# Moving the transposes of an attention kernel from TensorE to the DMA crossbar, and V's loads to another queue

## The chip, the cores and the metric

One core of a Trainium2 chip. The metric is the device time of one execution in microseconds (us). Each kernel was run several times, and the median is quoted. Runs that were flagged slow (over 1.5% above the fastest of the same kernel) are named where they occur and are left out of the ratios.

## The reference

Causal attention in which 16 extra "beacon" keys come before the 576 keys of each head, and then a two-layer MLP over all 4,608 tokens.

```python
B, H, S, Nb, D = 8, 8, 576, 16, 64          # q, k, v: [B, H, S, D], float32
k_all = concatenate([beacon_k, k], axis=2)
v_all = concatenate([beacon_v, v], axis=2)
scores = q @ k_all.T / sqrt(D)              # causal mask on the 576 keys only
a = softmax(scores)
x = (a @ v_all)  -> [B * S, H * D] = [4608, 512]
h = x @ w_in                                # 512 -> 2048
out = maximum(0.01 * h, h) @ w_out          # 2048 -> 512
```

## The kernel before

The program interleaves two kinds of work on TensorE. A *step* handles one pair of heads (32 pairs: 8 batches of 4): scores, exponentials on ScalarE, the product with V. *Fills* are pieces of the MLP that have their data already (MoE pieces). The order of each engine's instructions is fixed by the program; where an engine waits in the traces below, its later instructions wait too (DVE once for 24 us).

Q, K and the attention output must be transposed. Before, TensorE does that by multiplying with an identity, and DVE (VectorE) copies the result from PSUM, the memory into which TensorE writes, to SBUF, from which TensorE reads:

```python
def t_q(g, which, copy=nc.vector.tensor_copy):      # Q or K of pair g
    ...
    for i in range(RI):                              # 9 transposes
        nc.tensor.transpose(ps[:, i*RP:(i+1)*RP], nat[b, grp][which][ps_, i]..., ident[ps_, ps_])
    copy(out=dst..., in_=ps[:, 0:S]...)

def x_transposes(g):                                 # the attention output of pair g
    for t, (q0, rows) in enumerate(QT):              # 5 transposes
        nc.tensor.transpose(ps[:, q0:q0+rows], x_nat[0:rows, t]..., ident[0:rows, 0:rows])
    nc.vector.tensor_copy(out=xT[:, hp, b*S:(b+1)*S], in_=ps[:, 0:S])
```

The data comes in like this. Pool (GpSimd) issues the loads of Q and K and permutes them; SP issues V's loads and the stores of the result. Batch 2's loads stand behind 8 MB of MLP weights, and the step of pair 8 (the first of batch 2) has 16 extra fills ahead of its first transposes to cover that delay:

```python
def load_v(b, after=None):
    first = nc.sync.dma_start(out=t[0:NB, 0], in_=beacon_v[b]...)      # six DMAs on SP
    ...
def loads(g):
    ...
    if b > 1:
        if hp == 0: load_v(b + 1)
        if hp < 2:  load_qk(b + 1, hp)                 # Pool: 4 loads per group
    if hp >= 2:
        permute(b + 1, hp - 2, 0 and 1, Pool)
    if hp == 3: cast_v(b + 1, nc.gpsimd)
...
if g == 2 * NPAIR:                                     # pair 8
    ... finish(g - 1)
    for n in range(16): fill()
    t_q(g, 0); t_q(g, 1)
    ...
```

The softmax here doesn't subtract the row's maximum and nothing guards it: scores larger than these inputs give would overflow.

## Time and profile before

| | before |
|---|---|
| time, median of 4 runs | 375.11 us (374.99 to 377.84) |
| profiled span | 373.4 us |
| TensorE busy | 352.3 us, 94% |
| mean granted TensorE clock | 0.971 |

The page's rows below are those that the prediction does not show. The first gives each engine's busy time, its share of the span and its instructions; the other is the busy share of the DMA engines in 40 slices of the span, in tenths.

```profile
span 373.4 us, 7670 instructions
...
PE 352.3 (94%) x3215; PEld 186.8 (50%) x3264; DVE 172.3 (46%) x399; ACT 197.0 (53%) x311; POOL 101.3 (27%) x143
...
DMA  8998999939157900197017901100010011001012
```

TensorE is the bound. The DMA row has the shape that matters later: full for the first 75 us, and then a burst of one to three slices in each batch (the 7 9, 1 9 7, 1 7 9) with slices near zero between. In windows of the trace, the columns are the window, its length, the busy time of PE, PEld, DVE, ACT and POOL with instruction counts, the clock, the DMA share (the time of all packets over that of 16 engines; it can pass 1, because packets overlap) and GB/s.

```profile
48.00:75.00 27.00, 26.79 (x221) 13.81 (x223) 8.14 (x21) 13.37 (x22) 15.05 (x21) 1.00 1.17 210
...
205.00:219.00 14.00, 13.89 (x133) 7.08 (x133) 6.46 (x17) 11.04 (x20) 2.17 (x2) 1.00 0.70 127
```

In both windows TensorE is busy for all but 0.2 us or less at full clock, although the DMA engines are full in the first.

### The profile page before, as it was taken

Reading aid. Unit: us, or ns where it says so; the run is one execution under the profiler, and the core shown is the slowest. Engines: PE = TensorE matmul, PEld = TensorE weight load, DVE = VectorE, ACT = ScalarE, POOL = GpSimd, SP = SyncE. Lnnn points to the kernel's source line nnn. Section 1 sums busy time; section 2 is a strip of 40 time slices with the busy share of each in tenths; the row PEclk is TensorE's granted clock in tenths of the full one; section 3 lists DMA queues with packets and bytes.
Section 4 is the critical chain, followed back from the end, with each engine's and each line's share of the span. In section 5 each row is a group of like instructions: output and inputs, shape, how many; then the busy total and the mean of one; then the engine's idle time right before and its main releaser. Section 6 shows DMA issues by size and latency. Waiting matters only on the chain.

```text
span 373.4 us, 7670 instructions
## 1 busy us (share of the span) xinstructions
PE 352.3 (94%) x3215; PEld 186.8 (50%) x3264; DVE 172.3 (46%) x399; ACT 197.0 (53%) x311; POOL 101.3 (27%) x143
## 2 busy tenths in 40 slices
PE   5779899999998999999999999999999999999996
PEld 4456564445554555555554455455545554444442
DVE  3699750354558445654455535644554342000021
ACT  4949845476435773378535763587337701643300
POOL 8568127686014702370208101300000000000000
PEclk9558999999999999999999999999999999999999
DMA  8998999939157900197017901100010011001012
GB/s 173 172 221 128 200 203 203 223 81 155 56 126 174 177 0 30 58 152 135 2 59 131 184 2 57 58 2 2 36 50 31 0 58 58 0 5 53 28 56 84
DMA packets 58370, 33.82 MB, mean 91 GB/s; under 512 B 41440, under 2 KB 53472, under 8 KB 58336
## 3 DMA queue, kind: packets, MB, share of 16 engines
q0 software_dynamic: 13152, 13.34, 22.8%
q1 hardware_dynamic: 44896, 19.67, 21.4%
q8 instruction: 25, 0.41, 0.4%
q10 hardware_dynamic: 288, 0.33, 0.3%
q14 instruction: 9, 0.07, 0.1%
HBM read 37.22 MB, written 9.44 MB: 125 GB/s over the span
## 4 chain that ended last, share of the span: by engine, by line
PE 85%; DVE 6%; DMA 3%; POOL 2%; issue 2%; SPq 1%; ACT 0%; POOLq 0%
PE acc L385 33%; PE acc L369 33%; PE av L333 7%; PE sc L267 6%; PE tp L244 4%; PE tp L355 2%; DMA v_raw<-in_k_dram 1%; DMA v_raw<-in_v_dram 1%; DVE xT L360 1%; DVE osb L394 1%; DVE x_nat L343 1%; SPq L216 1%; DVE qT L249 1%; POOL k_raw L137 1%; DVE v_aug L225 1%
## 5 line engine op out<-in xcount | busy, mean ns | idle before, releaser
L369 PE MATMUL acc<-xT,w_in_sb 128*128 128x512 bf16 x552 | 137.6, 379 | 4.0 <-DVE xT L360 2.6
L278 ACT ACTIVATE aT<-sc 128x928 bf16<-128x928 f32 (+2 forms) x128 | 102.4, 856 | 71.4 <-PE sc L267 71.2
L385 PE MATMUL acc<-w_out_sb,gT 128*128 128x512 bf16 x551 | 134.5, 379 | 1.5 <-issue 0.8
L376 ACT ACTIVATE gT<-acc 128x512 bf16<-128x512 f32 x144 | 85.6, 599 | 81.9 <-PE acc L369 79.9
L369 PEld LDWEIGHTS <-w_in_sb 128*128 128x128 bf16 x576 | 52.3, 98 | 59.7 <-issue 4.5
L385 PEld LDWEIGHTS <-gT 128*128 128x128 bf16 x576 | 52.0, 98 | 59.9 <-issue 4.8
L394 DVE COPY osb<-acc 128x512 f32<-128x512 f32 x36 | 24.9, 690 | 95.6 <-PE acc L385 93.6
L333 PEld LDWEIGHTS <-aT 128*128 128x128 bf16 (+1 forms) x960 | 38.6, 100 | 19.0 <-issue 4.7
L267 PE MATMUL sc<-qT,kT 64*128 64x128 bf16 (+5 forms) x384 | 42.1, 306 | 5.0 <-ACT aT L278 2.6
L333 PE MATMUL av<-v_aug,aT 128*128 128x65 bf16 (+1 forms) x960 | 41.8, 197 | 2.5 <-DVE v_aug L225 1.9
L167 POOL COPY q_nat<-q_raw 128x1152 bf16<-128x1152 bf16 (+1 forms) x16 | 18.8, 1176 | 80.3 <-PE tp L244 69.2
L249 DVE COPY qT<-tp 128x576 bf16<-128x576 bf16 x32 | 24.2, 756 | 34.0 <-PE tp L244 33.9
L343 DVE TENSOR_TENSOR x_nat<-av,rec 128x384 bf16<-128x384 f32 x64 | 31.4, 491 | 2.2
L225 POOL CAST v_aug<-v_raw 128x512 bf16<-128x512 f32 (+1 forms) x30 | 19.0, 670 | 35.3 <-PE av L333 34.1
L360 DVE COPY xT<-tp 128x576 bf16<-128x576 bf16 x32 | 14.5, 452 | 29.3 <-PE tp L355 29.3
L267 PEld LDWEIGHTS <-kT 64*128 64x128 bf16 (+1 forms) x384 | 17.4, 100 | 20.5 <-issue 13.5
L342 DVE RECIPROCAL rec<-av 128x6 f32<-128x6 f32 x64 | 11.9, 185 | 29.9 <-PE av L333 29.9
L137 POOL DMA_DIRECT2D q_raw<-in_q_dram x31 | 19.4, 627 | 12.1 <-DMA v_raw<-in_v_dram 4.5
L299 DVE TENSOR_TENSOR aT<-aT,mask 128x768 bf16<-128x768 bf16 x32 | 21.1, 661 | 2.3 <-ACT aT L278 2.3
L137 POOL DMA_DIRECT2D k_raw<-in_k_dram x31 | 19.6, 631 | 8.4 <-DMA w_out_sb<-in_moe_w_out_dram 5.0
L249 DVE COPY kT<-tp 128x576 bf16<-128x576 bf16 x28 | 21.0, 749 | 0.0
L167 POOL COPY k_nat<-k_raw 128x1152 bf16<-128x1152 bf16 (+1 forms) x16 | 18.6, 1164 | 0.3 <-DMA k_raw<-in_k_dram 0.3
(33 smaller groups left out, 152.4 us busy)
## 6 DMA issues: line engine op xcount, KB each, us to landing
out_dram<-osb SPq DMA_DIRECT2D x36, 256.0 KB, 2.0
v_raw<-in_v_dram SPq DMA_DIRECT2D x24, 256.0 KB, 5.6
q_raw<-in_q_dram POOLq DMA_DIRECT2D x31, 144.0 KB, 6.0
k_raw<-in_k_dram POOLq DMA_DIRECT2D x31, 144.0 KB, 6.5
w_in_sb<-in_moe_w_in_dram POOLq DMA_DIRECT2D x4, 512.0 KB, 8.8
w_out_sb<-in_moe_w_out_dram POOLq DMA_DIRECT2D x4, 512.0 KB, 16.8
v_raw<-in_v_dram SPq DMA_DIRECT2D x8, 224.0 KB, 4.5
v_raw<-in_v_dram SPq DMA_DIRECT2D x8, 160.0 KB, 5.0
```

Source lines behind the costliest of these rows:

```text
L137: dma = nc.gpsimd.dma_start(out=dst[e * RP : (e + 1) * RP], in_=src[b, h0 : h0 + 2].rearrange("h (p i) d -> p h i d", i=RI),)
L167: copy(out=dst[p0:p1], in_=src[p0:p1].rearrange("p h i d -> p i h d"))
L225: eng.tensor_copy(out=dst[0 : ROWS[c], c, :, 0:D], in_=t[0 : ROWS[c], c])
L249: copy(out=dst.rearrange("c (p i) -> c p i", i=RI), in_=ps[:, 0:S].rearrange("c (i p) -> c p i", i=RI),)
L267: nc.tensor.matmul(out=sc[0 : ROWS[c], par, col - c0 : col - c0 + w], lhsT=kT[ps_, c * 128 : c * 128 + ROWS[c]], rhs=qT[ps_, q0 : q0 + w], ...
L278: last = nc.scalar.activation(out=aT[:, :, c0 : c0 + w], in_=sc[:, :, 0:w], func=AF.Exp, scale=0.125)
L333: nc.tensor.matmul(out=avv[:, n, 0 : D + 1], lhsT=aT[0 : ROWS[c], par, a0 : a0 + 128], rhs=va[0 : ROWS[c], c, 2 * hp + par, :], start=(c = ...
L343: nc.vector.tensor_tensor(out=x_nat[:, t0:t1].rearrange("p t e d -> p (t e) d"), in0=avv[:, :, 0:D], in1=rec[:, n0:n1, None].to_broadcast( ...
L369: nc.tensor.matmul(out=acc, lhsT=w_in_sb[:, j, fc * 128 : (fc + 1) * 128], rhs=xT[:, j, i * 512 : (i + 1) * 512], start=(j == 0), stop=(j ...
L376: nc.scalar.activation(out=gT[i][:, fc, :], in_=acc, func=AF.Prelu, alpha=0.01)
L385: nc.tensor.matmul(out=acc, lhsT=gT[i][:, fc, t * 128 : (t + 1) * 128], rhs=w_out_sb[:, fc, :], start=(fc == 0), stop=(fc == NF - 1),)
L394: nc.vector.tensor_copy(out=osb, in_=acc)
```

## The change

The intent is to take 522 transposes off TensorE. From batch 2 on, Q and K are transposed by DMAs through the crossbar (they transpose on the way from SBUF to SBUF), issued by SP right after Pool's permutes, into SBUF tiles from which DVE copies; so is the attention output of the first three pairs of each of these batches. V of batches 3 to 7 is loaded by ScalarE's queue, so that SP is free for the crossbar DMAs. The core of the diff:

```diff
-    def load_v(b, after=None):
+    def load_v(b, after=None, queue=nc.sync):
...
+    def turn_pairs(b, grp):
+        for which, name in enumerate(("q_turn", "k_turn")):
+            t = turnpool.tile([128, RI, 2, RP], BF16, name=name)
+            nc.sync.dma_start_transpose(out=t..., in_=nat[b, grp][which]...)
+        turned[b, grp] = tiles
+
+    def in_order(g, eng):
+        eng.tensor_copy(out=kT[:, 0:NB], in_=bkT[:, b, hp])
+        for t, dst in zip(turned[b, grp], (qT, kT[:, NB : NB + S])):
+            eng.tensor_copy(out=dst..., in_=t[:, :, e]...)
...
+    def x_turn(g):
+        nc.sync.dma_start_transpose(out=dst[:, None, 0:112], in_=flat[0:112, 0])
+        nc.sync.dma_start_transpose(out=dst[:, 112:496]..., in_=flat[:, 1:4]...)
+        nc.sync.dma_start_transpose(out=dst[:, None, 448:576], in_=flat[:, 4])
...
-                        load_v(b + 1)
+                        load_v(b + 1, queue=nc.scalar)
...
                     for which in range(2):
                         permute(b + 1, hp - 2, which, nc.gpsimd.tensor_copy)
+                    turn_pairs(b + 1, hp - 2)
...
+            if g + 1 >= 2 * NPAIR and has(g + 1):
+                in_order(g + 1, nc.vector)        # at the head of step g
...
-            x_transposes(g)
+            if b < 2 or hp == NPAIR - 1:
+                x_transposes(g)
+            else:
+                x_turn(g)
...                                                # and the t_q calls from pair 8 on are gone
```

The diff also changes numbers of buffers, which are not shown: four to three for the raw Q and K, three to two for the permuted ones, two to three for the attention output.

More of the change, by code (lines that the diff above doesn't have):

```diff
@@ L69 @@
     rawpool = ctx.enter_context(tc.tile_pool(name="rawpool", bufs=2))
-    qkpool = ctx.enter_context(tc.tile_pool(name="qkpool", bufs=4))
-    natpool = ctx.enter_context(tc.tile_pool(name="natpool", bufs=3))
+    qkpool = ctx.enter_context(tc.tile_pool(name="qkpool", bufs=3))
+    natpool = ctx.enter_context(tc.tile_pool(name="natpool", bufs=2))
+    turnpool = ctx.enter_context(tc.tile_pool(name="turnpool", bufs=2))
     headpool = ctx.enter_context(tc.tile_pool(name="headpool", bufs=2))
@@ L205, in behind @@
         )
-    def load_v(b, after=None):
+    def load_v(b, after=None, queue=nc.sync):
         t = rawpool.tile([128, NKB, H, D], FP32, name="v_raw")
         v_raws[b] = t
-        first = nc.sync.dma_start(out=t[0:NB, 0], in_=beacon_v[b].rearrange("h p d -> p h d"))
+        first = queue.dma_start(out=t[0:NB, 0], in_=beacon_v[b].rearrange("h p d -> p h d"))
         if after is not None:
             behind(first, after)
-        nc.sync.dma_start(out=t[NB:128, 0], in_=v[b, :, 0:112].rearrange("h p d -> p h d"))
+        queue.dma_start(out=t[NB:128, 0], in_=v[b, :, 0:112].rearrange("h p d -> p h d"))
         for c in (1, 2, 3, 4):
-            last = nc.sync.dma_start(
+            last = queue.dma_start(
                 out=t[0 : ROWS[c], c],
@@ L252, in t_q @@
         )
+    turned = {}
+    def turn_pairs(b, grp):
+        tiles = []
+        for which, name in enumerate(("q_turn", "k_turn")):
+            t = turnpool.tile([128, RI, 2, RP], BF16, name=name)
+            nc.sync.dma_start_transpose(
+                out=t.rearrange("c i e p -> c i (e p)"),
+                in_=nat[b, grp][which].rearrange("r i h d -> r (i h d)"),
+            )
+            tiles.append(t)
+        turned[b, grp] = tiles
+    def in_order(g, eng):
+        b, hp = divmod(g, NPAIR)
+        grp, e = divmod(hp, 2)
+        qT = headpool.tile([128, S], BF16, name="qT")
+        kT = headpool.tile([128, NB + S], BF16, name="kT")
+        eng.tensor_copy(out=kT[:, 0:NB], in_=bkT[:, b, hp])
+        for t, dst in zip(turned[b, grp], (qT, kT[:, NB : NB + S])):
+            eng.tensor_copy(
+                out=dst.rearrange("c (p i) -> c p i", i=RI),
+                in_=t[:, :, e].rearrange("c i p -> c p i"),
+            )
+        qk[g] = [qT, kT]
     probs = {}
@@ L319, in value @@
             xs[g] = (
-                headpool.tile([128, 5, 2, D], BF16, name="x_nat"),
+                headpool.tile([128, 5, 2, D], BF16, name="x_nat", bufs=3),
                 headpool.tile([128, 10], FP32, name="rec"),
@@ L360, in x_transposes @@
         nc.vector.tensor_copy(out=xT[:, hp, b * S : (b + 1) * S], in_=ps[:, 0:S])
+    def x_turn(g):
+        b, hp = divmod(g, NPAIR)
+        x_nat, _ = xs.pop(g)
+        flat = x_nat.rearrange("p t e d -> p t (e d)")
+        dst = xT[:, hp, b * S : (b + 1) * S]
+        nc.sync.dma_start_transpose(out=dst[:, None, 0:112], in_=flat[0:112, 0])
+        nc.sync.dma_start_transpose(
+            out=dst[:, 112:496].rearrange("p (t q) -> p t q", t=3),
+            in_=flat[:, 1:4].rearrange("p t x -> p (t x)"),
+        )
+        nc.sync.dma_start_transpose(out=dst[:, None, 448:576], in_=flat[:, 4])
     gT = {}
@@ L519 @@
                     fill()
-                t_q(g, 0)
-                t_q(g, 1)
-                fill()
-                fill()
                 score(g, 0)
@@ L528 @@
                 fill()
-                t_q(g + 1, 0)
-                t_q(g + 1, 1)
                 score(g, 2)
@@ L579 @@
             slot(3)
-            if has(g + 1) and g + 1 != 2 * NPAIR:
-                t_q(g + 1, 0)
-                t_q(g + 1, 1)
             if has(g):
```

## The prediction

> **What bounds the kernel now.** I read the page first: the rows by slice and the chain that ended last.
>
> ```profile
> PE   5779899999998999999999999999999999999996
> ACT  4949845476435773378535763587337701643300
> PEclk9558999999999999999999999999999999999999
> PE 85%; DVE 6%; DMA 3%; POOL 2%; issue 2%; SPq 1%; ACT 0%; POOLq 0%
> ```
>
> From about 45 us on (slice 5 of 9.3 us) TensorE is at 90% or more of nearly every slice, and 85% of the chain is PE. ScalarE is half idle on average but reaches 7 and 8 in some slices. So removing instructions from TensorE should pay one for one, if nothing new makes it wait. Next, the timeline of TensorE in the steady part, for what the transposes cost in place: their listed durations overlap, so I take start to start.
>
> ```profile
> 183.04 0.43 PE L244 MATMUL tp<-ident,q_nat 64*128 64x64 bf16 x9
> 183.31 0.34 PE L244 MATMUL tp<-ident,k_nat 64*128 64x64 bf16 x6
> ...
> 183.57 0.50 PE L267 MATMUL sc<-qT,kT 64*128 64x336 bf16 x7
> ...
> 189.51 0.44 PE L355 MATMUL tp<-ident,x_nat 112*128 112x112 bf16 x5
> 189.79 0.38 PE L385 MATMUL acc<-w_out_sb,gT 128*128 128x512 bf16 x1
> ```
>
> Eighteen Q/K transposes hold TensorE from 183.04 to 183.57, 0.53 us; five output transposes from 189.51 to 189.79, 0.28 us. One pair's step is 9.8 us (scores start at 168.5 and 178.3).
>
> Then the timeline around the change-over from batch 1 to batch 2, because the change moves the use of batch 2's data there:
>
> ```profile
> 43.72 0.28 DVE L305 TENSOR_TENSOR aT<-aT,mask 80x256 bf16<-80x256 bf16 x1
> 43.99 0.20 DVE L342 RECIPROCAL rec<-av 128x6 f32<-128x6 f32 x1
> 44.22 0.56 DVE L343 TENSOR_TENSOR x_nat<-av,rec 128x384 bf16<-128x384 f32 x1
> ...
> 47.49 0.72 PE L355 MATMUL tp<-ident,x_nat 112*128 112x112 bf16 x10
> ...
> 56.05 6.76 SPq L216 DMA_DIRECT2D v_raw<-in_v_dram  x4
> 57.06 1.15 POOL L167 COPY q_nat<-q_raw 128x1152 bf16<-128x1152 bf16 x1 [1.05 <-DMA q_raw<-in_q_dram]
> 58.14 1.16 POOL L167 COPY k_nat<-k_raw 128x1152 bf16<-128x1152 bf16 x1
> ...
> 67.81 0.43 PE L244 MATMUL tp<-ident,q_nat 64*128 64x64 bf16 x9
> ```
>
> Batch 2's Q and K exist in SBUF, permuted, only at 58.2 and 59.3 us; they queue behind 8 MB of weights. The kernel before covers that delay with sixteen MoE pieces and transposes Q and K only at 67.8 us. And DVE stands at the masks of pair 6 at 43.7 us, then goes straight to the division of pair 5, which TensorE needs at about 47.8 us (the second five of the ten output transposes at 47.49).
>
> **What the Trainium skill says.** "VectorE: DVE Perf Modes", The three transpose paths: a 128x128 transpose takes 390 ns on TensorE and 1309 ns by the DMA crossbar. That is latency; this trace shows 29 ns (0.53/18) and 56 ns (0.28/5) of TensorE's stream per transpose, so only the small number is to be saved. "TensorE: Matmul & The Clock Gate", Architectural detail: ScalarE and VectorE queues are strict first in, first out; only TensorE pulls weight loads ahead. The trace agrees as far as it shows: DVE's instructions run in program order. The same page, Part 1: TensorE idle for a window of about 3.4 us falls to half clock. The PEclk row shows 5 in slices 1 and 2, where PE is busy only 7 tenths. "DMA: Bandwidth & Descriptors", Issuing engines are not separate DMA queues: a DMA issued elsewhere runs on the same 16 engines, so moving V saves only the issuer's time, and costs the new issuer that time. The trace shows how large that time can be:
>
> ```profile
> 162.01 0.85 SPq L216 DMA_DIRECT2D v_raw<-in_v_dram  x1
> 162.91 4.15 SPq L216 DMA_DIRECT2D v_raw<-in_v_dram  x1
> 167.12 3.46 SPq L216 DMA_DIRECT2D v_raw<-in_v_dram  x1
> ```
>
> **The change, part by part.**
>
> 1. TensorE loses 24 pairs x 0.53 = 12.7 us and 18 pairs x 0.28 = 5.0 us: -17.8 us. The built programs confirm the counts: 1,044 fewer rows on TensorE, that is 522 transposes with their weight loads (24 x 18 + 18 x 5).
>
> 2. DVE: the 48 copies of Q and K stay, now from SBUF instead of PSUM (about 0.75 us, same strides; I expect 0.6 to 0.75). Eighteen xT copies of 0.45 us go. DVE is 46% busy and stays under half. No gain on the path.
>
> 3. The crossbar: 24 transfers of 288 KB and 54 smaller ones. V's 256-byte packets cost 21.4% x 16 engines x 373 us / 44,896 = 28 ns of an engine each. If crossbar rows of 256 bytes cost the same (an estimate), one Q or K transfer is 1,152 rows / 16 x 28 ns = 2.0 us plus a landing of about 2 us (the stores' 2.0 us), and a batch's four, with the outputs' three, some 11 us of 39. It fits; and in the steady part a pair of them has a step of 9 us before DVE wants it.
>
> 4. The new wait, which I think decides it. In the built program's DVE order, pair 8's copies from the crossbar tiles stand at the head of step 7: directly after the masks of pair 6, before the division of pair 5. They wait for the transposes of batch 2's Q and K. DVE cannot pass them. So DVE stops at about 44 us and TensorE at the weight load of pair 5's output transposes, about 47.8 us. When is K there? Pool's permutes end at 58.2 and 59.3 as before, for the weights' traffic sets them. On SP the transposes stand behind V of batch 2, whose issue ended at 56.05 + 6.76 = 62.8. The 16 engines are full then:
>
> ```profile
> 60.00:72.00 12.00, 11.95 (x72) 5.36 (x72) 2.19 (x4) 5.21 (x9) 9.97 (x15) 1.00 1.11 205
> ```
>
> From 55.2 us (weights landed) they must still move four Q/K loads of 144 KB, V of batch 2 (1.18 MB), part of V of batch 3 (ScalarE reaches its issue early; say 0.8 MB) and two transposes of 288 KB: 0.6 + 1.2 + 0.8 + 0.6 = 3.2 MB at the row's 205 GB/s, 15.6 us, so K lands near 70.5 us. Then K's copy 0.75, two reciprocals and two divisions 0.2 + 0.56 + 0.17 + 0.42 us: TensorE goes on at about 72 us. Loss: 72 - 47.8 = +24 us. Everything after it is TensorE's own stream, so it shifts whole.
>
> 5. Clock after 24 us of idling: one window at half clock, 3.4 us / 2 = +1.7 us.
>
> 6. V on ScalarE: six DMA issues at the head of the first pair's step of a batch. On SP one such load held the queue from 161.05 to 171.6 us, but SP ran ahead, into the Q/K loads of Pool; on ScalarE it comes two steps later, when the DMA engines are nearly idle. 1.18 MB at 16 x 256 B / 28 ns = 146 GB/s would be 8 us, at 205 GB/s 5.8; [...]ScalarE is held 4.5 to 6 us. The exponentials of scores 0 (1.02 us) come after that, and TensorE wants their PSUM back 4.4 us into the step: 1.5 us lost, for four batches (4 to 7; batch 3's falls into the stall): +6 us.
>
> 7. Small bubbles after 48 us (TensorE waited 1.2 us for xT at 121 us, DVE's kT 0.3 us) may go: -1.5 us.
>
> Sum: -17.8 + 24 + 1.7 + 6 - 1.5 = +12.4 us; 375.2 + 12.4 = 387.6, called 387 us.
>
> **The rivals.**
>
> A. TensorE saves its 17.8 us and nothing waits: 357 us. For it: 85% of the chain is PE and the steady part has a step of slack. Against it: in-order DVE and data that comes no earlier than 59.3 us. Even if K landed 3 us after Pool's permute, TensorE would go on only at 64 us: 16 us lost against 17.8 saved, 373 to 376 us.
>
> B. The crossbar is far slower than a copy: a Q/K pair needs over 9 us, DVE waits once or twice a batch for it, and everything behind it on SP (stores) is late. At 5 us per transfer K lands near 76 us and each of five batches loses 1 to 3 us: about 400 us. Nothing in this trace shows a crossbar transfer, so it cannot be excluded.
>
> C. ScalarE held by V becomes the largest loss: if the issue takes the 10 us that it took on SP, TensorE loses 6 to 7 us in each of four batches: 405 us. Against it: the Q/K loads are over by then.
>
> D. V's issue is short (under 3 us) and hidden: 381 us.
>
> **Range and chances.** The saving is sure within 1 us. The stall is 16 us at the very least and may be 30 with a slow crossbar; V costs 0 to 14 us. Most combinations lie in 379 to 398 us. Faster than 367.7 us would need the stall not to exist, which the order on DVE rules out unless data comes 15 us earlier: 0.03. Within 2% (367.7 to 382.7) needs a stall of under about 20 us or a free V: 0.24. Slower: 0.73.
>
> **What will show it.** The timeline should show DVE with nothing from 44 us to nearly 70 us, its qT copy ended by a DMA into q_turn, and TensorE idle from 47.8 to about 72 us; slices 5 to 7 of the PE row near 0, with PEclk low after them. In the steady part steps of about 9.0 us against 9.8; idle of ScalarE's exponentials or of TensorE's scores once a batch at the V issue. The row of the crossbar issues gives size and landing: 4 us supports step 3, 8 or more rival B. I am wrong if TensorE has no gap before 75 us, or if the steady step doesn't shorten by 0.5 us or more.

## The result, and the profile after

| | before | after |
|---|---|---|
| median of 4 runs each | 375.11 us | 410.95 us (405.84 to 411.99, one flagged slow) |
| ratio of fast runs | 1 | 1.089 (95%: 1.078 to 1.101) |
| profiled span | 373.4 us | 408.8 us |
| clock in the profiled run | 0.971 | 0.916 |

Ratios here and below are the mean time of one kernel's fast runs over that of the other's of the same rounds on the same chip, so not quite the ratio of the medians. The changed kernel is slower by 9%, more than the prediction's upper end of 398 us. The rows of its page:

```profile
span 408.8 us, 6822 instructions
...
PE 347.4 (85%) x2742; PEld 172.8 (42%) x2742; DVE 156.9 (38%) x381; ACT 195.5 (48%) x311; POOL 107.7 (26%) x143
...
PE   4678700799999879899967999499999999999996
...
PEclk9558965799999889999996999699999999999999
DMA  8999999944547279637992499528102102100112
...
PE 65%; DMA 20%; SPq 3%; DVE 3%; POOL 3%; ACT 2%; ACTq 2%; issue 1%; POOLq 0%
```

A slice is 10.2 us here. The PE row has a hole in slices 6 and 7 (the 0 0; the prediction counts slices from zero), which was predicted, and dents at slices 14 and 15, 21 and 22, and 26, which were not predicted at that depth. PEclk dips in or just after each of them. The chain of work that ended last is 65% PE against 85% before, and 20% DMA against 3%.

The hole first. DVE's timeline (start, length, operation, and in brackets how long the engine had been idle and what ended that):

```profile
45.55 0.16 DVE L275 COPY kT<-bkT 128x16 bf16<-128x16 bf16 x1
69.67 0.67 DVE L277 COPY qT<-q_turn 128x576 bf16<-128x576 bf16 x1 [23.96 <-DMA q_turn<-q_nat]
72.29 0.64 DVE L277 COPY kT<-k_turn 128x576 bf16<-128x576 bf16 x1 [1.95 <-DMA k_turn<-k_nat]
```

TensorE's, at the same place:

```profile
49.11 0.44 PE L384 MATMUL tp<-ident,x_nat 112*128 112x112 bf16 x5
73.69 0.94 PE L384 MATMUL tp<-ident,x_nat 112*128 112x112 bf16 x5 [24.14 <-DVE x_nat L372]
```

DVE stands for 24 us in front of a copy of pair 8's Q, and TensorE stands for 24.1 us in front of the output transposes of pair 5, whose division DVE has not reached. That is the predicted stall, nearly to the microsecond. But ScalarE's timeline shows a second engine that stands still over the same time:

```profile
49.92 0.45 ACTq L215 DMA_DIRECT2D v_raw<-in_v_dram  x1
63.68 6.65 ACTq L217 DMA_DIRECT2D v_raw<-in_v_dram  x4
77.03 0.60 ACT L418 ACTIVATE gT<-acc 128x512 bf16<-128x512 f32 x1 [27.12 <-PE acc L411]
```

ScalarE issues V of batch 3: two DMAs at once, then nothing until 63.68, then four more until 70.3. Only then could it have done an activation. (The bracket names TensorE, which came last.) Whether that matters, the experiments must say.

Now the later dents, by the one at 211 us. ScalarE:

```profile
207.25 0.34 ACTq L212 DMA_DIRECT2D v_raw<-in_beacon_v_dram  x1
208.75 0.32 ACTq L215 DMA_DIRECT2D v_raw<-in_v_dram  x1
209.20 6.54 ACTq L217 DMA_DIRECT2D v_raw<-in_v_dram  x4
215.83 1.86 ACT L307 ACTIVATE aT<-sc 128x1024 bf16<-128x1024 f32 x2 [8.77 <-DMA xT<-x_nat]
```

TensorE, in the four batches in which ScalarE loads V of the next (called V's four holds below):

```profile
134.44 0.37 PE L296 MATMUL sc<-qT,kT 64*128 64x336 bf16 x4 [1.76 <-ACT aT L307]
...
173.46 0.37 PE L296 MATMUL sc<-qT,kT 64*128 64x336 bf16 x4 [1.93 <-ACT aT L307]
...
216.91 0.57 PE L296 MATMUL sc<-qT,kT 64*128 64x336 bf16 x4 [6.04 <-ACT aT L307]
...
261.62 0.57 PE L296 MATMUL sc<-qT,kT 64*128 64x336 bf16 x4 [5.84 <-ACT aT L307]
```

ScalarE's exponential ends an idle time of 8.77 us that is put down to a *crossbar transpose of the output*, which the exponential does not read. The link is the DMA issues between. In the built program, the DMAs of SP and ScalarE take their completion semaphores (counters that tell that a DMA has landed) from one set of eight in turn, and a DMA waits for the last use of its semaphore to complete: eight issues back, of either engine. Set beside the trace's landings, V of batch 6 reads (issue and landing are those of the DMA waited for):

```
V's DMA on ScalarE   waits for                     issued    landed
chunk 0              k_turn (SP), its semaphore    193.44    208.7
chunk 1              xT, first part                199.84    209.2
chunk 2              xT, second part               203.35    209.4
chunk 3              xT, third part                209.44    214.7
chunk 4              xT, first part, next pair     210.65    214.9
```

ScalarE's chunk 0 went out at 208.75 and chunk 1 at 209.20, each as its transpose landed, and the last left at 215.7. So ScalarE, and through it TensorE, waited for late crossbar DMAs here, and in the next batch (251 to 260 us). The two smaller holds are different:

```profile
133.36 3.10 ACT L307 ACTIVATE aT<-sc 128x1024 bf16<-128x1024 f32 x4 [7.73 <-DMA out_dram<-osb]
...
168.21 4.07 ACTq L217 DMA_DIRECT2D v_raw<-in_v_dram  x4
```

In the first, V's last DMA waited 3.99 us for a *store of the result* that SP had issued at 128.42, and another 0.92 us for an output transpose. In the second no DMA of V waited for a landing: issuing the six took from 167.26 to 172.28, 5.0 us. Why were the crossbar DMAs late? SP's queue:

```profile
186.70 1.33 SPq L262 DMA_TRANSPOSE q_turn<-q_nat  x1
188.12 1.32 SPq L262 DMA_TRANSPOSE k_turn<-k_nat  x1
...
190.41 2.93 SPq L262 DMA_TRANSPOSE q_turn<-q_nat  x1
193.44 6.35 SPq L262 DMA_TRANSPOSE k_turn<-k_nat  x1
...
203.35 1.25 SPq L398 DMA_TRANSPOSE xT<-x_nat  x1
209.44 1.12 SPq L402 DMA_TRANSPOSE xT<-x_nat  x1
```

The same 288 KB transposes that landed 3.3 and 3.2 us after their issue at 186.7 and 188.1 took 16.7 and 15.3 us at 190.4 and 193.4. What had come between is Pool's eight loads of the next batch's Q and K, all in flight beside them. The third output transpose (209.44) also waits for the second (203.35) to land, 6.03 us later, because they write overlapping columns.

The two windows of before, in the changed kernel:

```profile
48.00:75.00 27.00, 2.80 (x39) 1.89 (x36) 3.31 (x9) 1.66 (x4) 14.06 (x20) 0.61 1.27 215
...
205.00:219.00 14.00, 7.70 (x50) 3.27 (x49) 4.10 (x8) 4.70 (x8) 4.68 (x4) 0.83 0.82 141
```

The whole difference of the profiled spans, +35.4 us, splits up as follows. Gaps of TensorE are those over 0.15 us, and the cost of the clock is half of the time in which TensorE was busy while the records give it half clock, each against the kernel before.

| part | us |
|---|---|
| the early hole: 24.1 gap, 1.9 clock | +26.1 |
| V's four holds: 17.0 gaps, 5.3 clock | +22.3 |
| before 47 us (1.4 gaps, 0.8 clock) | +2.2 |
| one wait for a copy of xT at 147.5 us (2.04 against 1.21 before), 1.6 clock | +2.4 |
| the rest, left over: the transposes that are gone | -17.6 |

The rest is close to what was promised for the transposes (-17.8), though it is a remainder and not measured by itself. A step without a hold runs from 223.57 to 232.59 us by its scores, 9.02 us, against 9.8 before.

### The profile page after: what moved, and what is told of

It reads as the page before. It is cut to its first block, busy times and chain, and to the rows that moved or that the text cites. A ratio compares the mean times of both kernels' runs of the same rounds, so it can differ in the third digit from the quotient of the medians.

```text
span 408.8 us, 6822 instructions
## 1 busy us (share of the span) xinstructions
PE 347.4 (85%) x2742; PEld 172.8 (42%) x2742; DVE 156.9 (38%) x381; ACT 195.5 (48%) x311; POOL 107.7 (26%) x143
## 4 chain that ended last, share of the span: by engine, by line
PE 65%; DMA 20%; SPq 3%; DVE 3%; POOL 3%; ACT 2%; ACTq 2%; issue 1%; POOLq 0%
PE acc L427 28%; PE acc L411 27%; DMA xT<-x_nat 7%; PE av L362 6%; PE sc L296 5%; DMA w_out_sb<-in_moe_w_out_dram 5%; DMA v_raw<-in_v_dram 3%; DMA k_raw<-in_k_dram 2%; SPq L217 2%; ACT aT L307 2%; DMA k_turn<-k_nat 1%; ACTq L217 1%; DMA v_raw<-in_k_dram 1%; DMA out_dram<-osb 1%; DVE osb L436 1%
## 5 line engine op out<-in xcount | busy, mean ns | idle before, releaser
L411 PE MATMUL acc<-xT,w_in_sb 128*128 128x512 bf16 x576 | 141.7, 383 | 3.4 <-DVE xT L389 3.4
L427 PE MATMUL acc<-w_out_sb,gT 128*128 128x512 bf16 x576 | 141.0, 385 | 0.0
L362 PEld LDWEIGHTS <-aT 128*128 128x128 bf16 (+1 forms) x960 | 41.2, 103 | 21.8 <-issue 8.6
L226 POOL CAST v_aug<-v_raw 128x512 bf16<-128x512 f32 (+1 forms) x30 | 23.8, 832 | 87.9 <-PE av L362 85.6
L362 PE MATMUL av<-v_aug,aT 128*128 128x65 bf16 (+1 forms) x960 | 44.3, 202 | 2.6 <-DVE v_aug L226 2.3
L168 POOL COPY q_nat<-q_raw 128x1152 bf16<-128x1152 bf16 (+1 forms) x16 | 20.1, 1254 | 59.8 <-DMA q_raw<-in_q_dram 35.9
L296 PEld LDWEIGHTS <-kT 64*128 64x128 bf16 (+1 forms) x384 | 15.4, 101 | 48.1 <-issue 42.9
L384 PE MATMUL tp<-ident,x_nat 128*128 128x128 bf16 (+1 forms) x70 | 6.9, 230 | 24.2 <-DVE x_nat L372 24.1
L277 DVE COPY qT<-q_turn 128x576 bf16<-128x576 bf16 x24 | 15.4, 643 | 24.0 <-DMA q_turn<-q_nat 24.0
L277 DVE COPY kT<-k_turn 128x576 bf16<-128x576 bf16 x24 | 15.5, 645 | 1.9 <-DMA k_turn<-k_nat 1.9
```

Of the source, the lines that this page charges most:

```text
L168: copy(out=dst[p0:p1], in_=src[p0:p1].rearrange("p h i d -> p i h d"))
L226: eng.tensor_copy(out=dst[0 : ROWS[c], c, :, 0:D], in_=t[0 : ROWS[c], c])
L277: eng.tensor_copy(out=dst.rearrange("c (p i) -> c p i", i=RI), in_=t[:, :, e].rearrange("c i p -> c p i"),)
L296: nc.tensor.matmul(out=sc[0 : ROWS[c], par, col - c0 : col - c0 + w], lhsT=kT[ps_, c * 128 : c * 128 + ROWS[c]], rhs=qT[ps_, q0 : q0 + w], ...
L362: nc.tensor.matmul(out=avv[:, n, 0 : D + 1], lhsT=aT[0 : ROWS[c], par, a0 : a0 + 128], rhs=va[0 : ROWS[c], c, 2 * hp + par, :], start=(c = ...
L411: nc.tensor.matmul(out=acc, lhsT=w_in_sb[:, j, fc * 128 : (fc + 1) * 128], rhs=xT[:, j, i * 512 : (i + 1) * 512], start=(j == 0), stop=(j ...
```

## The experiments

All kernels gave correct results. Each call had its own runs of the kernel before on its chip: medians 375.74 us for the first four, 377.11 for the next four, 376.62 for the last four.

### First call: which part makes the loss?

My theory after reading the trace: DVE's early copies make the hole, and V on ScalarE makes the later holds, because crossbar DMAs are late. **e1** moves the copies of pairs 8 and 9 behind the 16 fills, on DVE alone.

```diff
-            if g + 1 >= 2 * NPAIR and has(g + 1):
+            if g + 1 > 2 * NPAIR + 1 and has(g + 1):
                 in_order(g + 1, nc.vector)
...
                 for n in range(16):
                     fill()
+                in_order(g, nc.vector)
+                in_order(g + 1, nc.vector)
```

> Only the copies of pairs 8 and 9 out of the crossbar tiles are moved on DVE: from the heads of steps 7 and 8 to after the sixteen MoE pieces, where the kernel before transposed them. Theory: the 24.1 us gap of TensorE at 49.6 us and some 2 us of half clock after it go, the four later holds stay: 384 to 387 us. Rival (the start is bound by the loads, the wait only moves to the new place): 395 to 411 us, with a gap of 10 us or more between 50 and 80 us.

Measured: 400.91 us (398.45 to 402.76), ratio 1.066 (1.060 to 1.071). Only 10 us of 24 came back. DVE no longer waits, but TensorE still has this gap:

```profile
71.20 0.68 PE L384 MATMUL tp<-ident,x_nat 112*128 112x112 bf16 x5 [15.62 <-ACT gT L418]
```

and ScalarE's row, just before it, says why:

```profile
64.34 6.17 ACTq L217 DMA_DIRECT2D v_raw<-in_v_dram  x4
70.55 2.06 ACT L418 ACTIVATE gT<-acc 128x512 bf16<-128x512 f32 x4 [21.31 <-DMA q_turn<-q_nat]
```

The hole had two holders, and my theory had one. TensorE ran on for some 6 us in the fills, until it needed a PSUM buffer that ScalarE had not emptied.

**e2** undoes only V's move.

```diff
-                        load_v(b + 1, queue=nc.scalar)
+                        load_v(b + 1)
```

> Only V goes back to SP's queue. Theory: ScalarE is no longer held once a batch, so the 17 us of TensorE gaps after 130 us and the some 8 us of half clock around them go, the early gap stays: 384 to 388 us. Rival (SP, held by V's issue, brings the crossbar transposes late, and DVE or TensorE waits for those): 398 us or more, with waits of DVE for the crossbar tiles once a batch.

Measured: 396.6 us (395.6 to 398.76), ratio 1.056 (1.051 to 1.062). The hole stays (21.76 us, ended by DVE's division), which was expected. The holds of the scores are gone, but two waits that were not expected take their place: 5.85 us at 155 us and 3.56 us at 236 us, in which DVE waits for a crossbar tile of Q. The crossbar is late there too.

**e3** combines e1's and e2's edits.

> Both edits. Theory: losses add, so 357 to 363 us, faster than the kernel before by 3 to 5%. If the two losses share a cause, or SP's hold by V replaces ScalarE's: 370 us or more.

Measured: 376.58 us (370.02 to 379.56, two of four flagged slow), ratio of fast runs 0.991 (0.982 to 1.000); the theory's 357 to 363 us did not come. The early hole is gone: no gap over 1.2 us before 118 us. But one new wait costs over half of what the transposes save:

```profile
129.01 1.01 PE L411 MATMUL acc<-xT,w_in_sb 128*128 128x512 bf16 x2 [10.87 <-DMA xT<-x_nat]
```

SP's queue shows it to be the landing and the overlap together: the second output transpose went out at 121.12 and the third, which waits for it, only at 128.98.

```profile
121.12 1.26 SPq L398 DMA_TRANSPOSE xT<-x_nat  x1
128.98 1.11 SPq L402 DMA_TRANSPOSE xT<-x_nat  x1
```

**e7** is the opposite test: the kernel before, with nothing but V of batches 3 to 7 on ScalarE. No crossbar at all. If only late crossbar DMAs make ScalarE's issue slow, it must cost little.

```diff
-                        load_v(b + 1)
+                        load_v(b + 1, queue=nc.scalar)
```

> The kernel before with V of batches 3 to 7 on ScalarE's queue and nothing else: no crossbar transposes. Theory (ScalarE is held because V's issue waits for DMAs eight issues back, which in the changed kernel are late crossbar transposes): little to wait for here, 375 to 381 us. Rival (the length of V's issue itself holds ScalarE): 388 to 400 us, with TensorE gaps of 4 us or more in each of four batches.

Measured: 401.33 us (400.62 to 402.89), ratio 1.068 (1.064 to 1.072). My theory in its narrow form fell, and the rival's gaps of 4 us in each of four batches did not come either. V on ScalarE is worth 26 us by itself, and most of it is one hold. In TensorE's timeline:

```profile
68.74 0.68 PE L355 MATMUL tp<-ident,x_nat 112*128 112x112 bf16 x5 [14.28 <-ACT gT L376]
```

and in ScalarE's:

```profile
48.15 1.41 ACTq L214 DMA_DIRECT2D v_raw<-in_v_dram  x1
61.34 6.70 ACTq L216 DMA_DIRECT2D v_raw<-in_v_dram  x4
68.09 2.06 ACT L376 ACTIVATE gT<-acc 128x512 bf16<-128x512 f32 x4 [19.96 <-DMA v_raw<-in_v_dram]
```

Here the DMAs eight issues back are SP's loads of V of batch 2, behind the 8 MB of weights. In the later batches, with no crossbar about, no DMA of V waits for a landing. In the first of the four TensorE has no gap over 0.4 us; in the others the holds are 0.98, 1.95 and 1.81 us (with 0.46 us more each), about the 1.5 us of the prediction. So there are two findings: a DMA issue on a compute engine takes over the lateness of whatever stands eight issues back, and in the changed kernel's two large later holds that is the crossbar.

The 27.6 us between the profiled spans (401.0 and 373.4) can be followed through the weight loads, whose order is all but the same in both programs. Against the kernel before they start 0.7 us later at 52 us, 15.1 after the hole, and 17.2 from 73 us on; then 19.0, 21.8 and 26.1 after the three holds, and 27.5 from 253.7 us to the end. After the hole and after the last two holds some 1.5 to 2 us each are the clock: its record gives half clock at 59.3 to 72.9, 206.0 to 209.5 and 250.4 to 253.8 us. The mean clock of the run (0.970 against 0.971) hides this, because the kernel before has its half clock in the first 31 us; e7 ran those at full clock, and by 41 us it was not ahead.

### Second call: how much is each of these worth?

**e8** keeps e1's edit and leaves V of batch 3 alone on SP, so both early holders are gone and only the later holds stay.

```diff
-                        load_v(b + 1, queue=nc.scalar)
+                        load_v(b + 1, queue=nc.sync if b == 2 else nc.scalar)
```

> The copies of pairs 8 and 9 late, as in the first experiment, and V of batch 3 alone back on SP; V of batches 4 to 7 stays on ScalarE. Revised theory: the early gap has two holders side by side, DVE's copies of pair 8 and ScalarE's issue of V of batch 3, which waits for batch 2's loads; with both gone the gap goes and only the four later holds stay: 376 to 386 us, no gap over 3 us before 110 us. Rival (a third cause, such as the weights): 390 us or more.

Measured: 391.37 us (390.38 to 397.3, one flagged slow), ratio 1.038 (1.034 to 1.042). The early hole is gone: the largest gap before 107 us is 1.10 us. So e1 and e2, with one holder removed each, and e8 (as e3) with both removed, settle that it had two. The time itself lies in the rival's range; the missing gap tells the two apart. The later holds are larger than I had sized them: 7.82, 1.60, 4.44 and 5.36 us.

**e9** adds a cut of the output transposes in which no two write the same columns (112, 256, 80 and 128 columns, four DMAs). A cut that began at partition 48 could not be built.

```diff
-            out=dst[:, 112:496].rearrange("p (t q) -> p t q", t=3),
-            in_=flat[:, 1:4].rearrange("p t x -> p (t x)"),
+            out=dst[:, 112:368].rearrange("p (t q) -> p t q", t=2),
+            in_=flat[:, 1:3].rearrange("p t x -> p (t x)"),
         )
+        nc.sync.dma_start_transpose(out=dst[:, None, 368:448], in_=flat[0:80, 3])
```

> As the run above, and the outputs' transposes cut so that no two write the same columns of xT (112, 256, 80 and 128 columns, four DMAs for three): SP no longer waits for a landing inside them. If that wait is what makes the transposes late that ScalarE's V waits for: 4 to 10 us faster than the run above. Rival (the landing itself, slowed by Pool's Q/K loads, decides): within 3 us of it.

Measured: 385.42 us (382.46 to 387.93), ratio 1.023 (1.017 to 1.029; unclear at 2%). Six us less than e8, as expected: the wait for an overlapping write was a part of the holds, and not the whole. 5.60, 3.76, 1.36 and 5.46 us are left.

**e10** is e8 with the outputs transposed on TensorE again, so that SP has only the Q and K transposes.

```diff
-            if b < 2 or hp == NPAIR - 1:
+            if True:
                 x_transposes(g)
```

> As the first run of this call, with all outputs transposed on TensorE again (18 x 0.28 = 5 us more there) and only Q and K by the crossbar. If the outputs' transposes are what V's issue on ScalarE waits for, the later holds shrink to the 1 to 2.4 us each of the run with V alone moved: 368 to 375 us. Rival (Q's and K's transposes hold it): the first run plus 5 us.

Measured: 380.16 us (377.78 to 383.01), ratio 1.012 (1.006 to 1.018). It is 11 us faster than e8 though TensorE does some 5 us of work more; that is half right, for I had expected 368 to 375. The holds fall to 3.85, 1.16, 1.23 and 1.53 us (with 0.46 us more each), the last three the size of e7's; none of V's DMAs waits for a landing now. In the first, one issue took 6.36 us while Pool's loads and the Q and K transposes were in flight. So the output transposes made most of what held V on ScalarE in the steady part.

**e4** puts V of batches 3 to 7 on Pool's queue, with e1's edit. No compute on TensorE's path waits behind V's issue then.

```diff
-                        load_v(b + 1, queue=nc.scalar)
+                        load_v(b + 1, queue=nc.gpsimd)
```

> The copies of pairs 8 and 9 late, V of batches 3 to 7 on Pool's queue, so that neither ScalarE nor SP carries it. Theory: no holds: 357 to 365 us, the fastest so far. Rival (V's descriptors or bytes delay Q and K or the transposes as much): 370 us or more, with waits of TensorE for xT or of DVE for the crossbar tiles.

Measured: 377.61 us (371.16 to 384.04, two of four flagged slow), ratio of fast runs 0.990 (0.983 to 0.996). The holds are gone, and the lateness of the crossbar itself comes to the surface. TensorE:

```profile
144.80 1.17 PE L362 MATMUL av<-v_aug,aT 128*128 128x65 bf16 x18 [9.63 <-DVE x_nat L372]
```

DVE, which was to make that x_nat:

```profile
143.40 0.65 DVE L277 COPY kT<-k_turn 128x576 bf16<-128x576 bf16 x1 [9.14 <-DMA k_turn<-k_nat]
```

and SP:

```profile
124.03 5.03 SPq L262 DMA_TRANSPOSE k_turn<-k_nat  x1
129.16 10.17 SPq L262 DMA_TRANSPOSE q_turn<-q_nat  x1
```

The K transpose of 124.03 landed at 143.4, 19.4 us later, with Pool's loads of V, Q and K in flight beside it. By itself such a transpose takes 3.3 us.

### Third call: keep Pool's loads away from the crossbar

If Pool's loads make the crossbar late, holding them back until a batch's transposes have landed should free it, at no cost, for the loads have most of a batch to come in. **e12** is e4 with this gate; Pool issues in order, so the Q and K loads behind V wait too.

```diff
+            last = nc.sync.dma_start_transpose(...)
...
+        landed[b, grp] = last
...
-                        load_v(b + 1, queue=nc.gpsimd)
+                        load_v(b + 1, after=landed[b, 1] if b > 2 else None, queue=nc.gpsimd)
```

> As the run with V on Pool, and one more dependency: Pool starts V and the Q/K loads of batches 4 to 7 only when the last Q/K transpose of the batch before has landed. Theory (a crossbar transpose of 288 KB lands in some 3.5 us alone and in 11 to 19 us beside Pool's loads, and that is what the 9.6 us gap waits for): Q/K transposes all under 6 us after 80 us, the gap gone, 357 to 366 us and steadier between rounds. Rival (the loads now come too late, or the crossbar is slow by itself in that place): 370 us or more.

Measured: 363.53 us (363.11 to 364.37, all fast), ratio 0.967 (0.964 to 0.970). The theory held. Since half of e4's runs were flagged slow, the ratios of fast runs are to be compared: 0.990 to 0.967, 2.3 points or some 9 us from that one dependency (the two were run on different chips). SP's queue at the place where e4 stalled, as its counterpart above:

```profile
122.28 1.34 SPq L263 DMA_TRANSPOSE q_turn<-q_nat  x1
123.71 1.45 SPq L263 DMA_TRANSPOSE k_turn<-k_nat  x1
125.26 1.30 SPq L263 DMA_TRANSPOSE q_turn<-q_nat  x1
126.67 1.39 SPq L263 DMA_TRANSPOSE k_turn<-k_nat  x1
```

and Pool, which waits 10.7 us for the fourth of them and loses nothing by it:

```profile
130.55 0.55 POOL L212 DMA_DIRECT2D v_raw<-in_beacon_v_dram  x1 [10.71 <-DMA k_turn<-k_nat]
```

The four landed in 3.84, 3.44, 3.36 and 3.29 us, and from then on no Q or K transpose took over 4.7 us. TensorE's rows on the page:

```profile
PE   4878899799999699999999999999999999999995
...
PEclk9999899999999899999999999999999999999999
```

The largest gaps left after 47 us are 2.23 us at 68 us (DVE's copy of pair 8's K) and 3.00 us at 117.5 us (an output transpose).

**e13** is e3 with the same gate on Pool's Q and K loads, V on SP.

```diff
-                        load_qk(b + 1, hp)
+                        first_qk = load_qk(b + 1, hp)
+                        if hp == 0 and b > 2:
+                            behind(first_qk, landed[b, 1])
```

> As the run with late copies and all V on SP, with the same dependency on Pool's Q/K loads alone. Theory: the 10.9 us gap before the MoE of batch 2, where TensorE waits for the outputs' transposes, shrinks to under 4 us: 360 to 368 us. Rival (SP's stores and V before the transposes cause it): unchanged, 370 us or more.

Measured: 367.78 us (367.11 to 369.51), ratio 0.979 (0.975 to 0.982; unclear at 2%, but within what was expected). The Q and K transposes from 80 us on take 4.6 us at most there too. The gate is worth 1.2 points by the ratios of e3 and e13, some 4.5 us; their intervals just overlap, so that size is uncertain. A wait of 5.40 us for an output transpose at 119.5 us stays.

**e14** is e12 with e9's cut.

> As the first run of this call, with the outputs' transposes cut without overlap (four DMAs for three). If SP's wait for a landing between them still costs: 2 to 6 us faster than the first run. Rival: within 2 us, or slower for the extra DMA.

Measured: 362.55 us (360.3 to 363.78), ratio 0.962 (0.957 to 0.967). It is 1 us below e12, and their runs overlap; with the crossbar free the overlapping write hardly matters. It is the fastest version that I have, 3.8% faster than before.

**e15** is e12 with the outputs transposed on TensorE.

> As the first run of this call, with the outputs transposed on TensorE (5 us more there), only Q and K by the crossbar. If the outputs' transposes still cost waits worth more than 5 us, this is faster than the first run; if they are free now, it is 3 to 6 us slower.

Measured: 368.12 us (366.56 to 368.86), ratio 0.978 (0.975 to 0.982; unclear at 2%). 4.6 us slower than e12, near the 5.0 us of TensorE's time that the prediction gave these 90 transposes. So on a free crossbar they cost nothing, where in e8 they cost 11 us more than they saved.

What stays open is *why* Pool's loads slow a crossbar transpose up to sixfold (8.1 to 19.4 us against 3.3). The changed kernel's window around the slow ones says what it was not:

```profile
190.00:209.00 19.00, 18.78 (x163) 9.05 (x162) 8.93 (x21) 13.28 (x23) 8.27 (x11) 1.00 1.25 125
```

The DMA engines are taken (share 1.25, more than the 1.17 of the kernel before while it loads the weights), but move only 125 GB/s, against 210 then. So it was not a matter of bytes, and a sum by bytes cannot find it. Beside loads of V from ScalarE alone, 13 of 16 output transposes of the changed kernel landed in 3.0 to 5.3 us, against mostly 2.2 to 2.4 with nothing beside them. No run varied the number or the size of the loads, nor took the Q and K loads off Pool's queue.

## Why the prediction was wrong

The direction and the largest single loss were right; 387 us was 24 us too low, and the range did not hold the result. By its own steps:

1. The saving on TensorE, -17.8 us: right. The accounting leaves -17.6; the step came down to 9.02 us.
2. DVE gains nothing on the path: right. Its 48 copies from crossbar tiles took 0.64 us each, within the 0.6 to 0.75 expected.
3. "It fits; and in the steady part a pair of them has a step of 9 us before DVE wants it": **failed**. Alone, a transpose lands in 3.3 us, better than the 4 us assumed. But the sum gave a transfer its time alone; with Pool's Q and K loads beside them, three pairs issued in the steady part took 8.1 and 12.5, 16.7 and 15.3, and 15.0 and 15.9 us. Rival B had a slow crossbar, but one that is always slow; it was slow only in company. DVE's later copies had their step of slack in the changed kernel, so the loss did not show there but in step 6.
4. The early stall, +24 us: right in size (24.1), in place and in the row that shows it. Part of the fit is luck: it began at 49.55 and ended at 73.69 us, each 1.7 us later than forecast, and K landed at 72.27 and not at 70.5 (the prediction's own sum, 55.2 + 15.6, gives 70.8). Incomplete in its cause: see 6.
5. The clock after it, +1.7 us: right (1.9).
6. V on ScalarE, "1.5 us lost, for four batches (4 to 7; batch 3's falls into the stall): +6 us": **failed, and this is the step that broke the number**: 22.3 us, 17.0 in gaps and 5.3 in clock. Two things were wrong. I took the issue as a cost of descriptors and bytes alone. That cost was right, 5.0 us of issue in the batch where nothing waited (4.5 to 6 were expected), and the gaps there were 1.93 and 0.46 us. What was left out is a wait, for the DMA eight issues back: a late crossbar transpose in the last two batches, which have 12.4 of the 17.0 us of gaps, a store in the first. And I left out the clock for small gaps: three of these four holds, 1.8 to 6.0 us, each came with 3.4 or 6.8 us of half clock, 5.3 us in all. e7 shows that without the crossbar the gaps come near the predicted 6 us (6.1), and that the clock would still have been missing. Rival C had the place and, in two batches, the size of a gap (6 to 7 us), but put it down to the length of the issue. "Batch 3's falls into the stall" was true of the sum, and it hid that this hold alone makes a 14 us hole (e1: 15.62, e7: 14.28).
7. The small bubbles, -1.5 us: did not go. The wait at xT was 2.04 us.

The sum: +16.3 for step 6, +2.2 before 47 us, +2.4 for the xT wait and +1.5 for the bubbles that did not go make up 22.4 of the 23.0 us by which the profiled spans' +35.4 exceeds the predicted +12.4.

## What to carry to other kernels

Moving work to a DMA engine moves its wait into every in-order queue that stands behind it: look in each engine's program order for the first instruction that needs the new transfer, and for every DMA issue on a compute engine ask what it must wait for before it may be issued. When two waits cover the same time, removing one shows the other (ratios to the kernel before: 1.089 with both, 1.066 with one gone, 1.038 with none), so price each alone. And a transfer that is quick when alone has to be timed in its neighbours' company: here one added dependency that kept loads away from the transposes was worth 9 us, and with it, with the early waits removed and with V on Pool's queue, the change went from 9% slower to 3 to 4% faster.

## What the Trainium skill lacked or had wrong

- "DMA: Bandwidth & Descriptors", Issuing engines are not separate DMA queues: it says that issuing from several engines saves only sequencer time, usually small. The section does not say what the issue can cost a compute engine that takes it over: here, with eight semaphores shared in turn, ScalarE stood until earlier DMAs had landed, also those of another engine, some 20 us once (19.96 in e7, 21.31 in e1) and 8.77 us at 207 us.
- "Advanced Engine Details and Errata", X-Bar Transpose (TRN2), calls transpose DMAs as fast as regular DMAs, and "DMA: Bandwidth & Descriptors", Rules for kernel authors, says that a transpose next to ordinary DMAs needs nothing. The second is a rule on correct results, and agrees with those of all runs. Neither section warns of the time: a 288 KB transpose landed in 3.3 us alone and in 8 to 19 us beside Pool's loads.
- "VectorE: DVE Perf Modes", The three transpose paths: 390 ns on TensorE and 1309 ns by the crossbar are for one block. What decided here were the rates in a stream: 29 and 56 ns of TensorE per transpose in the trace before, and 3.3 us for a crossbar DMA of nine 128x128 blocks.
- "TensorE: Matmul & The Clock Gate", Part 1, gives an idle window of about 3.4 us. The records agree with the length of the half-clock stretches (3.4, 6.8 us), but gaps much shorter brought one. Of TensorE's gaps after 47 us in the fourteen profiles, all 22 of 2.9 us or more did, 10 of the 21 from 1.36 to 2.80 us did (1.76 us at 132.7 us; not 1.93 us at 171.5 us, nor 2.80 us in e3), and no shorter one. So these runs give no sharp threshold.
